# Layer one's a and b products in Strassen's form, fed by a list scheduler in the builder

## The chip, the core and the metric

The kernel runs on one core of one Trainium2 chip. TensorE (PE) multiplies matrices; VectorE (DVE), ScalarE (ACT) and GpSimd (POOL) do elementwise work; SyncE (SP) issues the DMAs. Each engine works through its own instructions in the order in which the program has them and waits at semaphores for the others. The metric is the device time of one execution in microseconds.

## The reference

Three stages follow each other, all in float32:

```python
# attention: batch 4, 8 heads, 576 tokens, head width 64
scores = scale * q @ k.T
scores = where(scores >= max(scores) - tau, scores, -1e9)
attn   = exp(scores - max) / (sum + 1e-9);  x = attn @ v      # x: 2304 x 512
# layer one: d_ff 1536
a = x @ w_a;  b = x @ w_b;  x = (a * b) @ w_out               # 2304 x 512
# layer two: d_ff 1024
h = x @ w_in;  sm = exp(h - max(h)) / sum;  s = h * sm
x = ((s - mean(s)) / sqrt(var(s) + 1e-6) * g_ln) @ w_out
```

## The kernel before

Every large float32 product runs in a rounded format that TensorE takes at one column per clock. Each operand is held as a high part (a rounded copy, made on ACT) and a low part (the operand minus the high part, made on DVE or POOL), and a product is the sum of three matmuls: high by high, high by low, low by high. So the a and b products of 128 features and n tokens are 2 x 4 x 3 = 24 matmuls n columns wide, and the y product (w_out) 4 x 3 = 12.

**Attention** runs in 72 steps of two score tiles, and six more in which the last tiles are worked off. A step's DVE scales the scores and takes their minimum (`ns`, L343), ACT takes the exponential (L355), POOL makes the threshold (`th`, L360), DVE masks and sums (L369), PE transposes (L389) and multiplies by v (L420). Single operations of other work are put between these by hand: the conversion of the first 15 weight pieces of 128x512 (L132, L135, L138 on DVE, L128 and L142 on ACT, the low part L145 on POOL), and the scaling and splitting of the first block of x. The x rows go to DRAM (`xd`) and come back by block.

**Layer one** walks over units of one token block by one block of 128 features (`units`, L644): four blocks of 512 tokens and one of 256 by twelve feature blocks, in two passes of six features. Per unit PE does the 24 a and b matmuls into one PSUM tile (`ab_mm`, L262) and the 12 y matmuls of the unit two before (`yacc`, L632, `LAG`). ACT copies a (L615), DVE multiplies by b (L616), ACT and DVE split the product (L617, L618). At the end of a pass ACT or DVE takes y out of PSUM (L636, L638); between the passes y waits in DRAM (`ypd`), x is stored once as `xsd` and read back and split again for the second pass. The remaining weight pieces are converted between the units in a fixed pattern (L661 to L666), and so are the 16 pieces of layer two.

**Layer two** takes 18 tiles of 128 tokens: `hid` (24 matmuls, L716), `chain` (softmax and variance on DVE and ACT), `lnt` (8 transposes L753, then L757 to L759) and `outp` (24 matmuls, L772). The input tiles are split on ACT and POOL (L594, L595).

Of the kernel before, what the change touches and what calls it, by code (L numbers as in the profile page):

```python
# [8 lines left out]
F32 = mybir.dt.float32  # L9
# [12 lines left out]
def kernel(  # L22
# [27 lines left out]
    NB = SM  # L50
    BLK = [[(b, 0, SM, 0)] for b in range(B)]
    BLK.insert(B - 1, [(b, SM, D, b * D) for b in range(B)])
    NBLK = len(BLK)
    LEN = [sum(n for _, _, n, _ in blk) for blk in BLK]
    TILES = [(j, c) for j in range(NBLK) for c in range(0, LEN[j], P)]
    NTILE = len(TILES)
    NW = 9
    F1 = 6
    LAG = 2
    RB = 2  # L60
    FW = 5
# [9 lines left out]
    xsd = [dram.tile([P, KC, n], F32, name=f"xsd{j}") for j, n in enumerate(LEN)]  # L71
    ypd = [dram.tile([P, KC, n], F32, name=f"ypd{j}") for j, n in enumerate(LEN)]
    yd = [dram.tile([P, KC, n], F32, name=f"yd{j}") for j, n in enumerate(LEN)]

# [9 lines left out]
    wstage = ctx.enter_context(tc.tile_pool(name="ws", bufs=2))  # L84
    xr_p = ctx.enter_context(tc.tile_pool(name="xr", bufs=1))
    xh_p = ctx.enter_context(tc.tile_pool(name="xh", bufs=1))
    ps_s = ctx.enter_context(tc.tile_pool(name="ps_s", bufs=2, space=PSUM))
    xs = {}
    vs = {}
    vnew = []  # L90
    pre = {}
    later = []
    xhs = [xh_p, None]
    wst = {}
    pools = {True: wpool}
# [24 lines left out]
    def conv_ops(stage):  # L120
        k = conv["k"]
        raw = conv["raw"].pop(k)
        n = raw.shape[1]
        w = {}

        def expo():
            w["f"] = stage.tile([P, n], F32, tag="w32", name="w32")
            nc.scalar.activation(out=w["f"], in_=raw[:, :, 1].bitcast(F32), func=AF.Abs, scale=2.0**-112)  # L128

        def low():  # L130
            w["l"] = stage.tile([P, n], U32, tag="wlow", name="wlow", bufs=1)
            nc.vector.tensor_scalar(out=w["l"], in0=raw[:, :, 0], scalar1=29, scalar2=None, op0=ALU.logical_shift_right)  # L132

        def sign():
            nc.vector.scalar_tensor_tensor(out=w["l"], in0=raw[:, :, 1], scalar=0x80000000, in1=w["l"], op0=ALU.bitwise_and, op1=ALU.bitwise_or)  # L135

        def join():
            nc.vector.scalar_tensor_tensor(out=w["f"].bitcast(U32), in0=w["f"].bitcast(U32), scalar=3, in1=w["l"], op0=ALU.logical_shift_left, op1=ALU.bitwise_or)  # L138

        def hi():  # L140
            w["o"] = conv_q[k][0]()
            nc.scalar.activation(out=w["o"][0], in_=w["f"] if wide else raw, func=AF.Copy)  # L142

        def lo():
            nc.gpsimd.tensor_tensor(out=w["o"][1], in0=w["f"] if wide else raw, in1=w["o"][0].bitcast(F32), op=ALU.subtract)  # L145

        return ([("A", expo), ("D", low), ("D", sign), ("D", join)] if wide else []) + [("A", hi), ("P", lo)]

    def conv_emit(stage, engs, count=1):
        while count and conv["k"] < min(conv["ld"], conv["lim"]):  # L150
            if not conv["ops"]:
                conv["ops"] = conv_ops(stage)
            if conv["ops"][0][0] not in engs:
                return
            conv["ops"].pop(0)[1]()
            count -= 1
            if not conv["ops"]:
                conv["k"] += 1

    def conv_step(stage):  # L160
        conv_load(stage)
        k = conv["k"]
        while conv["k"] == k and conv["k"] < conv["ld"]:
            conv_emit(stage, "ADP")

    def queue_w1(f):
        def piece(p):
            if p == 0:
                wst[f] = pools[f % NW < FW].tile([P, 3, 2, DM], F32R, tag="w", name=f"w1_{f}")
            return wst[f][:, p, 0], wst[f][:, p, 1]  # L170

        conv_pieces(piece, [w1[f, :, m] for m in range(3)])

    def queue_w2(i):
        def piece(p):
            g, p = divmod(i, 3)
            if p == 0:
                w2s[g] = pools[(NF + g) % NW < FW].tile([P, 3, 2, DM], F32R, tag="w", name=f"w2_{g}")
            return w2s[g][:, p, 0], w2s[g][:, p, 1]

        conv_pieces(piece, [w_in[:, i // 2, (i % 2) * 512:(i % 2 + 1) * 512] if i < 2 * KC else w_out[:, i - 2 * KC]])

    def load_x(j):
        n = LEN[j]
        xr = xr_p.tile([P, KC, NB], F32, name="xr0")[:, :, 0:n]
        zr = xr_p.tile([P, KC, NB], F32, name="zr")[:, :, 0:n]
        for b, s0, m, c in BLK[j]:
# [5 lines left out]
            for h in range(2):  # L193
                zs = rzd[b].rearrange("(k h) s -> h k s", h=2)[h:h + 1, :, s0:s0 + m]
                nc.sync.dma_start(out=zr[h * D:(h + 1) * D, :, c:c + m], in_=zs.to_broadcast([D, KC, m]))
        xs[j] = (xr, zr)

    def new_xt(j):
        return xhs[j % 2].tile([P, KC, 2, NB], F32R, name="xt")[:, :, :, 0:LEN[j]]

    normed = set()

    def norm_x(j, e):
        while vnew:
            b = vnew.pop()
            nc.vector.tensor_scalar(out=vs[b], in0=vs[b], scalar1=neg, scalar2=EPS / S, op0=ALU.mult, op1=ALU.mult)
        xr, zr = xs[j][:2]
        for b, _, m, o in BLK[j]:
            xe = xr[:, e, o:o + m]
            nc.vector.scalar_tensor_tensor(out=xe, in0=xe, scalar=vs[b][:, e, 0:1], in1=zr[:, e, o:o + m], op0=ALU.add, op1=ALU.mult)  # L210
        normed.add((j, e))

    def prep_x(j, st):
        if st == 0:
            xs[j] += (new_xt(j),)
        xr, zr, xt = xs[j]
        if st == 0:
            for e in range(KC):
                if (j, e) not in normed:
                    norm_x(j, e)  # L220
        for c in range(0, KC, 2):
            k = slice(c, c + 2)
            x0 = xr[:, k]
            if st == 0:
                nc.scalar.activation(out=xt[:, k, 0, :], in_=x0, func=AF.Copy)
            else:
                nc.vector.tensor_tensor(out=xt[:, k, 1, :], in0=x0, in1=xt[:, k, 0, :].bitcast(F32), op=ALU.subtract)
        if st == 1:
            later.append(lambda: nc.sync.dma_start(out=xsd[j], in_=xr))
            xs[j] = xt  # L230

    def prep_slots(j):
        xr, zr = xs[j]
        xt = new_xt(j)

        def high(e):
            nc.scalar.activation(out=xt[:, e, 0, :], in_=xr[:, e], func=AF.Copy)

        def low(e):
            nc.vector.tensor_tensor(out=xt[:, e, 1, :], in0=xr[:, e], in1=xt[:, e, 0, :].bitcast(F32), op=ALU.subtract)  # L240
            if e == KC - 1:
                later.append(lambda: nc.sync.dma_start(out=xsd[j], in_=xr))
                xs[j] = xt

        slots = []
        for c in range(0, KC, 2):
            slots += [(lambda e=e: norm_x(j, e), lambda e=e: high(e)) for e in range(c, c + 2)]
            slots += [(lambda e=e: low(e), None) for e in range(c, c + 2)]
        return slots

    def ab_mm(j, f):
        n = LEN[j]
        xt = xs[j]
        wt = wst[f]
# [18 lines left out]
    def prep_x2(j, c):  # L273
# [4 lines left out]
        if c + 2 == KC:  # L278
            xs[j] = xt
# [594 lines left out]
```

## Time and profile before

| | |
|---|---|
| time of three runs | 934.35, 933.31, 934.26 us; median 934.26 |
| the profiled execution | span 931.8 us (first to last instruction); 2.5 us below the median of the runs |
| attention | 0 to about 265 us |
| layer one | 264.88 to 711.92 us |
| layer two | 711.92 to 931.8 us |
| matmul instructions in the trace | 5680 |
| DMA | 95.46 MB, mean 102 GB/s |

The page gives the busy share of each engine over the span and in 40 slices, the clock that TensorE was granted, and the chain of work that ended last. The ends of matmuls are modelled, so a single matmul's duration is not its share of the time: what a matmul costs in a dense stream is the length of a piece of the chain divided by its count. Operations on the vector engines are read from their mean duration by shape.

### The profile page before, as it was taken

The page shows a single profiled execution, that of the slowest core. Times are in us where ns is not written, and L with a number is a line of the kernel's source. Part 1 is how long each engine was busy: PE and PEld are TensorE (multiplying, and loading weights), DVE is VectorE, ACT ScalarE, POOL GpSimd, SP SyncE. Part 2 cuts the span into 40 slices and gives each one's busy share as a digit, 9 for nine tenths or more (in the row PEclk, how much of TensorE's full clock was granted, in tenths as well). Part 3 has the DMA queues.
Part 4 walks back from the last instruction along what each step waited for, and adds up shares of the span by engine and source line. Part 5 has one row for each costly group of instructions (what it writes and reads, how often), then busy time and mean ns, then how long its engine had stood idle before and what let it go on. Part 6 is the DMA issues. An engine that isn't in the chain of part 4 may idle for free.

```text
span 931.8 us, 15032 instructions
## 1 busy us (share of the span) xinstructions
PE 919.4 (99%) x5680; PEld 704.5 (76%) x5680; DVE 538.2 (58%) x1169; ACT 438.5 (47%) x795; POOL 209.4 (22%) x292
## 2 busy tenths in 40 slices
PE   7999999999999999999999999999999999999998
PEld 3655555555578888889888888889988788888886
DVE  6999999999855243433266762223365544444443
ACT  5888888888743133333235432112232444444432
POOL 1233332333101002020023320000032433333330
PEclk9999999999999999999999999999999999999999
DMA  6445653367114334253126551122052111111100
GB/s 186 140 126 167 190 176 113 115 197 215 39 35 154 88 113 101 104 136 136 46 66 208 177 182 45 45 91 79 13 181 68 35 46 46 46 46 46 45 24 34
DMA packets 52904, 95.46 MB, mean 102 GB/s; under 512 B 12768, under 2 KB 29280, under 8 KB 50272
## 3 DMA queue, kind: packets, MB, share of 16 engines
q1 hardware_dynamic: 52032, 93.82, 31.9%
q8 instruction: 45, 0.74, 0.3%
q10 hardware_dynamic: 800, 0.68, 0.3%
q14 instruction: 27, 0.22, 0.1%
HBM read 70.80 MB, written 23.68 MB: 101 GB/s over the span
## 4 chain that ended last, share of the span: by engine, by line
PE 91%; DVE 5%; issue 1%; ACT 1%; DMA 0%; POOL 0%; ACTq 0%; POOLq 0%; DVEq 0%
PE ps L262 32%; PE py L632 16%; PE po L772 10%; PE ps L716 9%; PE po L420 8%; PE ps L338 7%; PE tp L389 7%; DVE ns L343 2%; PE pl L753 2%; DVE pe L369 1%; PE tq L405 1%; DVE e L728 0%; ACT e L727 0%; DMA taub<-in_tau_dram 0%; DVE nm L724 0%
## 5 line engine op out<-in xcount | busy, mean ns | idle before, releaser
L262 PE MATMUL ps<-xt,w 128*128 128x512 f32 (+1 forms) x1440 | 305.6, 368 | 0.0
L262 PEld LDWEIGHTS ps<-xt,w 128*128 128x128 f32 x1440 | 251.5, 189 | 45.0
L632 PE MATMUL py<-gt,w 128*128 128x512 f32 (+1 forms) x720 | 157.3, 368 | 0.0
L616 DVE TENSOR_TENSOR g<-ps,a 128x512 f32<-128x512 f32 (+1 forms) x60 | 38.3, 638 | 203.1 <-ACT a L615 203.1
L632 PEld LDWEIGHTS py<-gt,w 128*128 128x128 f32 x720 | 126.3, 189 | 22.5
L145 POOL TENSOR_TENSOR w<-w,w 128x512 fp32r<-128x512 f32 x52 | 76.9, 1479 | 283.5 <-ACT w L142 281.4
L615 ACT ACTIVATE a<-ps 128x512 f32<-128x512 f32 (+1 forms) x60 | 33.2, 554 | 193.0 <-PE ps L262 193.0
L355 ACT ACTIVATE pe<-ns,nm 128x576 f32<-128x576 f32 x128 | 94.0, 775 | 39.8 <-DVE ns L343 39.4
L343 DVE TENSOR_SCALAR_CACHE_REDUCE ns<-ps 128x576 f32<-128x576 f32 x144 | 103.0, 750 | 4.6 <-PE ps L338 4.4
L716 PE MATMUL ps<-w,ys 128*128 128x512 f32 x432 | 102.7, 393 | 1.6 <-POOL ys L595 1.4
L369 DVE SCALAR_TENSOR_TENSOR pe<-ns,th,pe 128x576 f32<-128x576 f32 x128 | 100.3, 813 | 5.1 <-ACT pe L355 2.8
L772 PE MATMUL po<-w,lt 128*128 128x512 f32 x432 | 101.4, 390 | 0.7 <-POOL lt L759 0.6
L338 PE MATMUL ps<-k,q 64*64 64x288 f32 x1152 | 90.8, 424 | 5.3 <-DMA k<-in_qkv_dram 3.4
L772 PEld LDWEIGHTS po<-w,lt 128*128 128x128 f32 x432 | 80.8, 188 | 18.1 <-POOL lt L759 1.1
L716 PEld LDWEIGHTS ps<-w,ys 128*128 128x128 f32 x432 | 79.8, 188 | 18.1 <-POOL ys L595 1.8
L360 POOL TENSOR_SCALAR th<-nm,toff 128x1 f32<-128x1 f32 x144 | 55.2, 386 | 157.2 <-DVE ns L343 152.2
L382 ACT ACTIVATE pt<-tp 128x512 f32<-128x512 f32 (+1 forms) x160 | 77.8, 545 | 0.7 <-PE tp L389 0.6
L420 PE MATMUL po<-pt,vr 128*64 128x322 f32 (+1 forms) x512 | 76.9, 419 | 0.5 <-ACT pt L382 0.4
L389 PEld LDWEIGHTS tp<-ident,pe 128*128 128x128 f32 x512 | 56.5, 143 | 23.8 <-issue 8.8
L389 PE MATMUL tp<-ident,pe 128*128 128x128 f32 x512 | 72.1, 280 | 0.2
L420 PEld LDWEIGHTS po<-pt,vr 128*64 128x64 f32 x512 | 32.2, 136 | 40.4 <-issue 17.2
L338 PEld LDWEIGHTS ps<-k,q 64*64 64x64 f32 x1152 | 36.9, 134 | 33.0 <-DVE ns L343 6.8
(74 smaller groups left out, 805.2 us busy)
## 6 DMA issues: line engine op xcount, KB each, us to landing
wraw<-in_w_dram SPq DMA_DIRECT2D x36, 512.0 KB
q<-in_qkv_dram SPq DMA_DIRECT2D x15, 576.0 KB
k<-in_qkv_dram SPq DMA_DIRECT2D x30, 176.0 KB
xd<-xp SPq DMA_DIRECT2D x16, 289.0 KB
y<-yd SPq DMA_DIRECT2D x18, 256.0 KB
vr<-in_v_dram SPq DMA_DIRECT2D x16, 256.0 KB
xr<-xd SPq DMA_DIRECT2D x4, 1024.0 KB
zr<-rzd SPq DMA_DIRECT2D x8, 512.0 KB
```

The source lines that it names most:

```text
L145: nc.gpsimd.tensor_tensor(out=w["o"][1], in0=w["f"] if wide else raw, in1=w["o"][0].bitcast(F32), op=ALU.subtract)
L262: nc.tensor.matmul(pa[:, 0:n], lhsT=wt[:, m, wi, kc * P:(kc + 1) * P], rhs=xt[:, kc, xi, :], start=(k == 0), stop=(k == 3 * KC - 1))
L338: nc.tensor.matmul(ps[t * D:(t + 1) * D, g, 0:HS], lhsT=q[r, u, c], rhs=k[r, u, o:o + HS], start=True, stop=True, skip_group_check=True)
L343: nc.vector.tensor_scalar(out=ns, in0=st[i, s][:, :, 0:HS], scalar1=-SCALE, scalar2=None, op0=ALU.mult, op1=ALU.min, accum_out=nm)
L355: nc.scalar.activation(out=pe.rearrange("p (g s) -> p g s", g=2), in_=ns, func=AF.Exp, bias=nm, scale=-1.0)
L369: nc.vector.scalar_tensor_tensor(out=pv, in0=ns, scalar=th, in1=pv, op0=ALU.is_le, op1=ALU.mult, accum_out=z[:, s:s + 1])
L382: evac_q.append(lambda: nc.scalar.activation(out=out, in_=in_, func=AF.Copy))
L389: nc.tensor.transpose(tp[:, kc, :], pe[:, o:o + P], ident)
L420: nc.tensor.matmul(po[h * D:(h + 1) * D], lhsT=lhsT, rhs=rhs, start=(kc == 0), stop=(kc == NQ), skip_group_check=True)
L632: nc.tensor.matmul(py, lhsT=wt[:, 2, wi, oc * P:(oc + 1) * P], rhs=gt[:, gi, :], start=(first and k == 0), stop=(last and k == 2))
L716: nc.tensor.matmul(ph[:, g, :], lhsT=y[:, a, kc, :], rhs=w2(2 * kc + g, b), start=(k == 0), stop=(k == 3 * KC - 1))
L772: nc.tensor.matmul(po, lhsT=lt[:, a, j, :], rhs=w2(2 * KC + j, b), start=(k == 0), stop=(k == 3 * NJ - 1))
```

## The change

The tokens are regrouped into three pairs of two halves of 384 tokens (`H`), the features into four passes of three blocks (`F1`). A unit is one pair by one feature block; there are 36, and the pairs run forward in even passes and backward in odd ones (`PAIRS`), so that the pair at a turn is kept.

In a unit the 2x2 problem (a and b by two token halves, with x cut into two halves of 256 rows) is done with seven products in place of eight. Each is 6 matmuls of 384 columns. Products 0, 3, 5 and 6 accumulate in one PSUM bank, 1 and 4 in a second, product 2 alone in a third; between them ACT copies the partial sums out (L951, L1008) and DVE adds them up (L1001, L1011, L1020). The two results a*b of the halves come from L1012 and L1029 and are split as before (L1018, L1021, L1032, L1033). The seven x operands are sums and differences made once per pair (`sum_ops`, `operand_ops`), stored in DRAM (`opd`) and read back when the pair comes again (`load_op`). The seven weight operands per feature block are made from differences of the converted pieces (`ab_tasks`).

The order on the engines of layer one comes from a list scheduler in the builder: it keeps a clock per engine with costs (`COST`, 0.1735 us per matmul of 384 columns, L182), and before each operation of the fixed chain it places those background tasks that would end early enough (`bg`, `crit`). Product 0 and 1 of the next unit stand before product 6 of the present one, and 24 y matmuls are spread over the gaps. In layer two `ys` of tiles 1 and 2 is made ahead, and `lnt(0)` stands before `chain(1)`.

```diff
-    NW = 9
-    F1 = 6
-    LAG = 2
+    H = NT // 6
+    NPR = NT // (2 * H)
...
+    F1 = 3
+    NPASS = NF // F1
+    NU = NPASS * NPR * F1
+    PAIRS = [p if q % 2 == 0 else NPR - 1 - p for q in range(NPASS) for p in range(NPR)]
...
+    opd = [[dram.tile([P, QK, 2, H], F32, name=f"opd{p}_{j}") for j in range(7)] for p in range(NPR)]
...
+    COST = {"A": (0.19, 0.83e-3), "D": (0.155, 1.04e-3), "P": (0.17, 2.17e-3), "S": (0.4, 0.0)}
...
+    def place(e, n, ready, sbuf):
+        s = max(clock[e], ready)
+        z = s + COST[e][0] + COST[e][1] * n * (e != "S")
+        if sbuf and n and e in port:
+            z += max(0.0, port["P" if e == "D" else "D"] - s - 0.1)
+        return s, z
...
+    def bg(limit, free_d=0.0, free_a=0.0, slack=0.5):
+        ends = {"D": limit + max(slack, free_d), "A": limit + max(slack, free_a)}
+        tasks[:] = sorted((t for t in tasks if t["ops"]), key=lambda t: t["due"])
...
+                        if s <= limit if e in "SP" else z <= ends[e]:
+                            got.append((s, t))
...
+    def crit(e, n, ready, fn, sbuf=False):
+        bg(ready)
+        _, z = place(e, n, ready, sbuf)
+        fn()
...
+        td = task(due - 7, [
+            diff(512, lambda: t()[:, 0:2], lambda: a()[:, 1], lambda: a()[:, :, 0, :]),
+            diff(256, lambda: t()[:, 2], lambda: a()[:, 1, 1], lambda: t()[:, 0]),
+            diff(256, lambda: t()[:, 3], lambda: a()[:, 0, 1], lambda: t()[:, 2]),
+        ], [tb])
...
+    def operand_ops(s, j, p):
+        def src():
+            return scs[s][:, (0, 0, 0, 1, 3, 2)[j]] if j in (1, 3, 4, 5) else quad(p, j // 6, min(j // 2, 1))
...
+    def load_op(s, j, p):
+        xts[s, j] = new_xt(s, j)
+        nc.sync.dma_start(out=xts[s, j].bitcast(F32), in_=opd[p][j])
...
+    def product(n, f, j):
+        ps = bank_of(n, BANK[j])
...
+        for c in range(QK):
+            for wi, xi in ACC:
+                nc.tensor.matmul(ps, lhsT=w[:, WOP[j], wi, c * P:(c + 1) * P], rhs=x[:, c, xi, :], start=(k == 0 and j < 3), stop=(k == 3 * QK - 1 and j in (2, 4, 6)), skip_group_check=True)
+                k += 1
...
+            free[n + 1, 1, 2] = tz[0] = crit("D", H, max(e2, tz[0]), lambda: nc.vector.tensor_tensor(out=tmp[0], in0=y, in1=tmp[0], op=ALU.add))
...
+            y_mm(4)
+            e3 = product(n, f, 3)
+            free[n, 0, 5] = tz[1] = crit("A", H, e3, lambda: nc.scalar.activation(out=tmp[1], in_=x, func=AF.Copy))
+            work(n, 1)
+            e4 = product(n, f, 4)
...
+            e5 = product(n, f, 5)
+            free[n, 0, 6] = tz[2] = crit("D", H, max(e5, tz[2]), lambda: nc.vector.tensor_tensor(out=tmp[2], in0=x, in1=tmp[2], op=ALU.add))
...
+            y_mm(6)
+            if n + 1 < NU:
+                fn = (n + 1) // F1 // NPR * F1 + (n + 1) % F1
+                nxt = first_copies(n + 1, (product(n + 1, fn, 0), product(n + 1, fn, 1)) if n else e01)
+            work(n, 5)
+            e6 = product(n, f, 6)
...
-            if t + 1 < NTILE:
-                split_y(t + 1, yp)
+            for k in (1, 2) if t == 0 else (t + 1,) if 1 < t < NTILE - 1 else ():
+                split_y(k, yp)
...
-            if t == NTILE - 1:
+            if t in (1, NTILE - 1):
                 lnt(t - 1)
```

Three places show how the instructions move. First PE in the steady part of layer one: before, one unit of 512 tokens (`ps` is the PSUM tile of a and b, `xt` the x block, `py` the y bank, `gt` the split product).

```order
L262 MATMUL ps<-xt,w_3_2160 128x512 x24
L632 MATMUL py<-gt,w_1_1149 128x512 x12
L262 MATMUL ps<-xt,w_4_3011 128x512 x24
L632 MATMUL py<-gt,w_2_1626 128x512 x12
```

After, a little more than one unit of 768 tokens (`acc` are the banks of a unit's products, `ga` and `gb` the split results of its two halves).

```order
L510 MATMUL acc_3966<-xt,w_4_4737 128x384 x6
L510 MATMUL acc_3969<-xt,w_4_4737 128x384 x6
L933 MATMUL py_3847<-ga,wo_4754 128x384 x2
L933 MATMUL py_3847<-ga,wo_4852 128x384 x3
L933 MATMUL py_3847<-ga,wo_4902 128x384 x3
L933 MATMUL py_3844<-gb,wo_4754 128x384 x3
L933 MATMUL py_3844<-gb,wo_4852 128x384 x3
L510 MATMUL acc_3966<-xt,w_4_4737 128x384 x6
L933 MATMUL py_3844<-gb,wo_4902 128x384 x3
L933 MATMUL py_3845<-gb,wo_4754 128x384 x3
L510 MATMUL acc_3967<-xt_5237,w_5_5001 128x384 x6
L510 MATMUL acc_3969<-xt_5237,w_5_5001 128x384 x6
```

The long runs of 24 and 12 became pieces of 6 and fewer, and all matmuls are 384 columns wide: 1512 for the products and 864 for y, where 1440 and 720 stood. The eighth row is product 5, which adds to the bank that L1008 copies after product 3 (the first row).

Second, PE at the start of layer one: before, with the last PV matmuls of attention (`po`) and the first units.

```order
L262 MATMUL ps<-xt,w_1_1149 128x512 x24
L262 MATMUL ps<-xt,w_2_1626 128x512 x24
L632 MATMUL py<-gt,w_0_672 128x512 x12
L262 MATMUL ps<-xt,w_3_2160 128x512 x24
L632 MATMUL py<-gt,w_1_1149 128x512 x12
```

After, from the same place (`py` banks serve as product banks in unit 0).

```order
L510 MATMUL py_3847<-xt,w_1_1324 128x384 x6
L510 MATMUL acc_3969<-xt,w_1_1324 128x384 x6
L510 MATMUL py_3844<-xt,w_0_852 128x384 x6
L510 MATMUL py_3845<-xt,w_0_852 128x384 x6
L510 MATMUL py_3844<-xt,w_0_852 128x384 x12
L510 MATMUL acc_3968<-xt,w_1_1324 128x384 x6
L510 MATMUL py_3847<-xt,w_1_1324 128x384 x6
L510 MATMUL acc_3969<-xt,w_1_1324 128x384 x6
L510 MATMUL py_3847<-xt,w_1_1324 128x384 x6
```

In the first three units no y matmul stands between the products; the fifth row is products 5 and 6 of unit 0 with nothing between them.

Third, DVE in the last units of layer one: before, a unit's two operations and the conversions between them.

```order
L616 TENSOR_TENSOR g_7001<-ps,a_7000 128x512
L618 TENSOR_TENSOR gt<-g_7001,gt 128x512
L138 SCALAR_TENSOR_TENSOR w_6966<-w_6966,wlow 128x512
L132 TENSOR_SCALAR wlow<-wraw 128x512
L135 SCALAR_TENSOR_TENSOR wlow<-wraw,wlow 128x512
```

After, one unit (`c` are the partial sums, `sc` and `wraw` belong to a weight piece of layer two, L907 takes y out of PSUM).

```order
L1001 TENSOR_TENSOR c_7571<-acc_3968,c_7571 128x384
L1033 TENSOR_TENSOR gb<-c_7469,gb 128x384
L907 TENSOR_TENSOR y_7526<-py_3846,y_7526 128x384
L225 SCALAR_TENSOR_TENSOR sc<-sc 128x512
L1011 TENSOR_TENSOR c_7572<-acc_3969,c_7572 128x384
L1012 TENSOR_TENSOR c_7571<-c_7571,c_7572 128x384
L907 TENSOR_TENSOR y_7551<-py_3847,y_7551 128x384
L218 TENSOR_SCALAR sc<-wraw 128x512
L1020 TENSOR_TENSOR c_7573<-acc_3966,c_7573 128x384
L1021 TENSOR_TENSOR ga<-c_7571,ga 128x384
L907 TENSOR_TENSOR y_7602<-py_3844,y_7602 128x384
L221 SCALAR_TENSOR_TENSOR sc<-wraw,sc 128x512
```

A unit has seven DVE operations of its own in place of two, and the conversions and y sums stand one by one between them.

## Rows read from the trace of the kernel before

**Rows 1.** The page: busy us, share and instructions; granted TensorE clock in 40 slices.

```profile
PE 919.4 (99%) x5680; PEld 704.5 (76%) x5680; DVE 538.2 (58%) x1169; ACT 438.5 (47%) x795; POOL 209.4 (22%) x292
...
PEclk9999999999999999999999999999999999999999
```

**Rows 2.** Busy time by stage: window, length, engines' busy us, clock, DMA share, GB/s.

```profile
8.65:264.88 256.23, 255.56 (x2476) 149.13 (x2476) 245.50 (x660) 212.87 (x413) 73.56 (x157) 1.00 0.48 147
274.00:712.00 438.00, 438.00 (x2137) 371.44 (x2136) 192.22 (x295) 138.06 (x235) 60.14 (x39) 1.00 0.32 106
712.00:931.80 219.80, 213.30 (x1008) 176.47 (x1006) 96.69 (x203) 83.59 (x142) 73.97 (x84) 1.00 0.15 46
```

**Rows 3.** The chain of waits, layer one: start us, us, engine, tile, line, count.

```profile
264.88 5.67 PE ps L262 x24
270.55 2.86 PE po L420 x20
273.42 0.21 PE rt L441
...
295.40 5.44 PE ps L262 x24
300.84 2.72 PE py L632 x12
...
429.51 2.88 PE ps L262 x24
432.39 1.44 PE py L632 x12
...
711.92 5.45 PE ps L716 x24
```

**Rows 4.** Groups by shape, 274 to 712 us: count, busy us, mean ns, idle before.

```profile
L262 PEld LDWEIGHTS ps<-xt,w 128*128 128x128 f32 x1413 | 246.6, 189 | 44.0
L145 POOL TENSOR_TENSOR w<-w,w 128x512 fp32r<-128x512 f32 x37 | 57.6, 1557 | 255.3 <-ACT w L142 255.3
L138 DVE SCALAR_TENSOR_TENSOR w<-w,wlow 128x512 uint32<-128x512 uint32 x37 | 38.0, 1026 | 1.9 <-ACT w L128 0.5
L618 DVE TENSOR_TENSOR gt<-g,gt 128x512 fp32r<-128x512 f32 x48 | 33.3, 693 | 33.5 <-ACT gt L617 33.5
L616 DVE TENSOR_TENSOR g<-ps,a 128x512 f32<-128x512 f32 x48 | 33.2, 692 | 175.7 <-ACT a L615 175.7
L135 DVE SCALAR_TENSOR_TENSOR wlow<-wraw,wlow 128x512 uint32<-128x512 uint32 x37 | 25.6, 693 | 1.3
L132 DVE TENSOR_SCALAR wlow<-wraw 128x512 uint32<-128x512 uint32 x37 | 15.8, 427 | 1.2
L618 DVE TENSOR_TENSOR gt<-g,gt 128x256 fp32r<-128x256 f32 x12 | 5.1, 426 | 5.8 <-ACT gt L617 5.8
L616 DVE TENSOR_TENSOR g<-ps,a 128x256 f32<-128x256 f32 x12 | 5.1, 424 | 27.3 <-ACT a L615 27.3
```

**Rows 5.** Weight loads where all matmuls are 256 wide, 425 to 437 us.

```profile
L262 PEld LDWEIGHTS ps<-xt,w 128*128 128x128 f32 x72 | 8.9, 192 | 0.0
```

**Rows 6.** Waits of PE in layer two, 712 to 932 us: total us, times, longest.

```profile
PE ps L716 <- POOL ys L595: 1.4, 1, 1.4
PE po L772 <- POOL lt L759: 0.6, 1, 0.6
```

**Rows 7.** Groups by shape in attention, 0 to 265 us on DVE, to 275 on POOL.

```profile
L138 DVE SCALAR_TENSOR_TENSOR w<-w,wlow 128x512 uint32<-128x512 uint32 x15 | 10.2, 679 | 0.0
...
L145 POOL TENSOR_TENSOR w<-w,w 128x512 fp32r<-128x512 f32 x15 | 19.3, 1286 | 28.2 <-ACT w L142 26.1 <-DVE ns L343 2.1
```

**Rows 8.** Single microseconds with a store of long rows, and with x and rz loads.

```profile
330.00:331.00 1.00, 1.00 (x6) 0.85 (x5) 0.00 (x0) 0.42 (x1) 1.00 (x1) 1.00 0.94 393
331.00:332.00 1.00, 1.00 (x6) 0.80 (x6) 0.00 (x0) 0.00 (x0) 0.24 (x1) 1.00 0.97 393
410.00:411.00 1.00, 1.00 (x10) 1.00 (x10) 0.93 (x3) 0.64 (x2) 0.00 (x0) 1.00 1.07 207
```

More of the change, by code (lines that the diff above doesn't have):

```diff
@@ new lines, in place, with commit, ready_of, transfer @@
+    def place(e, n, ready, sbuf):
[4 more added lines that the diff above has]
+        return s, z
+    def commit(e, z, sbuf):
+        clock[e] = z
+        if sbuf and e in port:
+            port[e] = z
+    def ready_of(t):
+        return max([t["end"], slot_at.get(t["ops"][0][3], 0.0)] + [d["end"] for d in t["deps"]])
+    def transfer(z, mb):
+        clock["Q"] = max(clock["Q"], z) + mb / RATE
+        return clock["Q"] + 2.0
@@ L140, in hi @@
-        def hi():
[L141 to L187, printed above, removed]
+            f = w["f"].bitcast(U32)
+            nc.vector.scalar_tensor_tensor(out=f, in0=f, scalar=3, in1=w["l"], op0=ALU.logical_shift_left, op1=ALU.bitwise_or)
+        if wide:
+            return [("A", 512, expo), ("D", 300, low), ("D", 512, sign), ("D", 512, join)]
+        return [("A", 512, lambda: nc.scalar.activation(out=dst(), in_=got["raw"], func=AF.Copy))]
@@ new lines, in whole_task, with part @@
+    def whole_task(src, tile_of, due, at, b, deps=(), free=None):
+        ld = load_w(src, due - 10, at - 16 if free is None else free, free is not None)
+        got = {}
+        def part(k):
+            if "b" not in got:
+                got["b"] = buffer(b)
+            return got["b"][:, k * DM:(k + 1) * DM]
+        t = task(due - 6, stage_ops(ld["got"], lambda: part(0), lambda: part(1)), [ld["load"]] + list(deps) + ([last[b]] if b in last else []), at - 12)
+        ld["used"] = t
+        last[b] = task(due, split_ops(tile_of, lambda: part(0), 512), [t], at)
+        return last[b]
@@ L192, in load_x @@
                 vnew.append(b)
[L193 to L249, printed above, removed]
@@ new lines, with bank_of, y_bank @@
+    ACC = ((0, 0), (0, 1), (1, 0))
+    WOP = (0, 3, 1, 5, 2, 4, 6)
+    BANK = (0, 2, 1, 0, 2, 0, 0)
+    bank = {}
+    free = {}
+    def bank_of(n, b):
+        if n == 0:
+            return bank["y"][(0, 2, 1)[b]][:, 0:H]
+        if n == 1 and b == 0:
+            return bank["y"][3][:, 0:H]
+        if "m" not in bank:
+            bank["m"] = [pools["ps"].tile([P, 512], F32, name=f"acc{k}", tag="tp") for k in range(4)]
+        return bank["m"][n % 2 if b == 0 else b + 1][:, 0:H]
+    def y_bank(i):
+        return bank["y"][i % 4][:, 0:H]
@@ L680, in moe1, with flush @@
+        def flush(every=False):
             for fn in later:
@@ L697, in moe2, with rest @@
+        for fn in lag:
+            fn()
+        slot["c"] = SL * (NU + 1)
+        for c in range(SL * NU, SL * (NU + 1) + 1):
+            slot_at[c] = clock["PE"]
+        while ysteps:
+            y_mm(9)
+            bg(clock["PE"])
+            flush()
+        flush(True)
+        es.close()
+        es_s.close()
+    def rest(left=None):
+        slot["c"] = SL * (NU + 9)
+        for t in sorted(tasks, key=lambda t: t["due"]):
+            force(t)
+    def moe2():
         es = ExitStack()
```

715 lines of the change are left out of this document (505 added, 210 removed).

## The prediction

> **What bounds the kernel now.** I read the page first: PE is busy for 99% of the span, at the full clock in all 40 slices [rows 1]. Since the ends of matmuls are modelled, that alone proves little, so the stages come next. In attention PE is busy for 255.56 of 256.23 us and DVE for 245.50; in layer one PE for all of 438.00 and DVE for 192.22; in layer two PE for 213.30 of 219.80 [rows 2]. The chain of waits then shows that layer one is nothing but matmuls: pieces of 24 and of 12 follow each other without a gap until layer two begins at 711.92 [rows 3]. So PE sets the time, what PE is given to do in layer one is what the change alters, and DVE has room there (44% busy).
>
> **PE's work in layer one.** A matmul of 512 columns costs 5.44 / 24 = 226.7 ns, one of 256 columns 2.88 / 24 = 120.0 ns; the pieces of y give the same, 2.72 / 12 and 1.44 / 12 [rows 3]. Four blocks of 512 tokens and one of 256, twelve features, 24 + 12 matmuls: 1728 x 226.7 + 432 x 120.0 ns = 391.7 + 51.8 = 443.5 us. The chain has 711.92 - 264.88 - 2.86 - 0.21 = 444.0, so the account closes.
>
> The changed kernel has 36 units of 7 x 6 = 42 product matmuls and 24 y matmuls, 2376 in all, each 384 columns wide. That width is not in the trace. From below, it costs at least what a column costs at 512, 226.7 x 0.75 = 170.0 ns; from above, at most what a column costs at 256, 120.0 x 1.5 = 180.0 ns. The two widths fit a constant part of 13 ns and 0.417 ns a column, which gives 173.3 ns; I take it, since 384 lies between the two rows it rests on. 2376 x 173.3 = 411.8 us, **31.7 us less** (39.6 less by the lower bound, 15.8 by the upper). The y matmuls alone stay at the same number of columns; the gain is the eighth product.
>
> **What the change puts on DVE and POOL, and what hides it.** Own DVE work per unit: four operations that read PSUM, between 692 and 424 ns, so 558 ns at 384, and three in SBUF, between 693 and 426, so 560 [rows 4]; over 36 units 80 + 60 us. 72 y sums of 558 ns: 40 us. 46 weight pieces of 427 + 693 + 1026 ns [rows 4]: 99 us. Weight differences, low parts and x operands that the order leaves to DVE, 21 of 512 columns' length, 12 of 256 and some ten longer ones: about 29 us. Together 309 of 411.8 us, 75%. POOL has 82 operations in layer one, as much as 82 of 512 columns; at 1557 ns [rows 4] 128 us, 31%. PE covers both as long as a result is there when PE comes to it. The two short covers are these: product 5 follows product 3's copy (ACT) behind product 4 and 14 y matmuls, 20 x 173 ns = 3.5 us; product 6 follows L1020 behind 6 y matmuls and two products of the next unit, 18 x 173 ns = 3.1 us. The add of 0.56 us leaves 2.5 us of the shorter cover. So in the steady part I cost the longer chain of sums at nothing, and keep 3 us for single late results and late loads over 36 units (0 to 20).
>
> **The start of layer one loses cover.** In the first three units no y matmul stands between the products. In unit 0 product 6 comes right behind 5, so it waits for the add, 0.56 us and the release; product 5 waits for ACT's copy behind one product only. Queued behind those waits on PE is everything, so they count in full: about 0.8 + 0.4 us, and a few tenths in units 1 and 2. The second pair's operands go through POOL then: thirteen operations, four low parts of weights (5.5 us), then nine sums and low parts of 768 columns' length (1557 x 1.5 = 2.3 us), 26 us in a row, against some 20 us until unit 3's first product and 13 more until its last; the first operand is out after 15, the last after 26. I take 2 us (0 to 8).
>
> **Attention.** The same PE work in the same order stands there, and PE had 0.7 us to spare in 256 [rows 2], so nothing can be won. DVE gets less to do: 15 pieces of three conversions (30 us) become 6 pieces and 16 scalings. POOL gets 17 operations for the first weights and 11 long ones for x between the thresholds; the masks and the next tile's scores are their cover. I take 0, with a bound of +6 (half a microsecond at each of the long ones). The three products at its end (18 x 173 = 3.1 us, where 5.67 stood [rows 3]) still outlast ACT's last copies; then 2.86 of PV follow as before.
>
> **Layer two** has the same matmuls. PE's wait for `ys` of tile 2 (1.4 us and its weight load's part) and for `lt` of tile 0 (0.6) [rows 6] should go, since both are made earlier: -2 (-3 to +3, the latter if layer two's last weight pieces, which are converted during the last y matmuls, hold up the first chain).
>
> **The sum,** against the profiled execution: 931.8 - 31.7 + 2 + 3 - 2 = 903.1 us of span. The runs' median lies 2.5 us above that execution, so the prediction is **906 us**; 898 to 914 by the bounds of the terms as they come most often.
>
> **The rivals.**
> *Late data, 921 us.* Passes two to four move 42 x 0.786 MB of x operands, 144 x 0.197 MB of y and 34 x 0.524 MB of weights, 79 MB in 27 units of 11.4 us: 256 GB/s, where layer one had 106 [rows 2]. Long rows went at 393 GB/s, broadcast rz with x at 207 [rows 8]. The operands have rows of 6 KB and are like the former; even with all y traffic at 207 the queue has 267 us of work in 308. But an operand's buffer comes free only one unit before its successor is needed. Six changes of operands at 3 us each, in place of the 3 us above: 906 - 3 + 18 = 921. Chance 0.10.
>
> *DVE and POOL exclude each other, 928 us.* DVE's L138 takes 679 ns in attention and 1026 in layer one, POOL's L145 1286 and 1557 [rows 4, 7]: each POOL operation there cost DVE about 0.35 us, which over 82 makes 309 + 28 = 337 us, still under PE. If every POOL operation stopped DVE for its whole length, DVE would need 309 + 128 = 437 us, 25 more than PE, and the time would be 906 - 3 + 25 = 928. The operations that read PSUM (120 us of the 309) speak against it: at 692 ns L616 is no longer than its SBUF neighbour. Chance 0.07. The Trainium skill (SBUF — State Buffer, Who interferes with whom) has it that the port pair DVE shares with GpSimd is an exclusive lock held for the whole instruction. By that rule this rival gains; the trace agrees in kind, with 347 ns where the whole operation would be 1557.
>
> *Slower: DVE is late at product 6 in every unit, 942 us.* The place is L1020. If two conversions stand before it and the first is caught behind a long POOL operation, 2.3 + 0.69 + 1.03 + 0.56 = 4.6 us pass where the cover is 3.1. That is 1.5 us of waiting; in 26 of 36 units it is 39 us: 906 - 3 + 39 = 942. It decides against the change from 31.7 / 36 = 0.9 us a unit on. For it: the order has four conversion operations a unit on average. Against: with 75% load a backlog must clear within the unit. Chance 0.06.
>
> *The weight load sets the pace, 943 us.* A load of 128x128 shows 189 ns [rows 4], more than 173. At 189 ns a matmul layer one would take 449 us, 6 more than now: 934.3 + 6 + 2 + 3 - 2 = 943. Against it: where all matmuls are 256 wide the loads show 192 ns [rows 5] and yet a matmul comes every 120. Chance 0.03.
>
> **How the numbers follow.** The forecast has 0.74; the four rivals 0.10, 0.07, 0.06 and 0.03. Faster by more than 0.2%, which is about what the measurement can tell: the forecast and the first two, less some overshoot, 0.89. Slower 0.09, the rest 0.02. For the range I take 896 to 928: down to the lower bound of the matmul with layer two's gain, up to the two middle rivals.
>
> **What would show it.** Right: in layer one the chain is made of L510 in pieces of 6 at 1.04 us and L933, its length is 412 to 420 us, and PE's longest waits stand in its first three units; layer two is 218 us long and attention ends within 3 us of 265. Wrong: DVE or POOL in the chain of the steady part, L1020 as what PE waits for, waits for `xt` from `opd`, a granted clock below full in some slice, or a matmul of 384 columns that costs 180 ns or more in a dense stretch.

## The result and the profile after

The changed kernel takes **946.34 us** (median of 4 runs, 946.07 to 947.08) against 934.31 us before in the same runs: a ratio of 1.013, 95% interval 1.0115 to 1.0144. The forecast was 906 us, faster; the kernel is slower. The profiled execution has a span of 944.8 us, 13.0 more than before.

The page of the changed kernel, to be held against [rows 1]: PE busy is down by 10.9 us, and the clock is no longer full in every slice.

```profile
PE 908.5 (96%) x5896; PEld 752.5 (80%) x5896; DVE 654.3 (69%) x1359; ACT 471.9 (50%) x886; POOL 283.0 (30%) x347
...
PEclk9999999999999898999999999999999899999999
```

Busy time by stage, changed kernel, columns as in [rows 2]: attention up to the first product of layer one, layer one, layer two, and 260 us out of the middle of layer one.

```profile
8.65:279.02 270.37, 261.89 (x2475) 149.59 (x2476) 248.32 (x637) 208.88 (x399) 90.85 (x170) 0.99 0.48 146
279.02:719.30 440.28, 426.56 (x2402) 422.87 (x2398) 300.18 (x503) 174.43 (x339) 113.42 (x79) 0.98 0.68 235
719.30:944.80 225.50, 216.53 (x1009) 178.89 (x1008) 103.20 (x212) 85.78 (x146) 77.05 (x86) 0.98 0.14 45
380.00:640.00 260.00, 260.00 (x1492) 260.00 (x1491) 176.87 (x310) 100.51 (x198) 52.61 (x44) 1.00 0.69 236
```

Against the stages of before (264.88; 447.0; 219.9 us, [rows 2, 3]) attention has got 14.1 us longer, layer one only 6.8 shorter, layer two 5.6 longer. From 380 to 640 us nothing is wrong: PE never stops. The chain of waits there (start, us, engine, tile, line, count) consists of products and y pieces alone, one unit every 11.51 us (28 units from 371.94 to 694.34 us):

```profile
417.98 4.16 PE acc L510 x24
422.83 2.08 PE acc L510 x12
424.91 2.43 PE py L933 x14
429.42 4.22 PE acc L510 x24
```

So the loss sits in three places, and the list of PE's waits (us in total, times, longest) names them: the masks of attention (L617), four entries in the first six units of layer one, and `rz` at the start of layer two. Left out are the first loads and, but for the second entry of L1020, what stays under 1.2 us in total.

```profile
PE acc L510 <- DVE xt L448: 5.6, 2, 3.5
PE tp L637 <- DVE pe L617: 5.2, 7, 1.6
PE pl L1125 <- DVE rz L1106: 4.9, 2, 4.7
PE py L933 <- DVE wo L236: 4.6, 1, 4.6
...
PE py L510 <- DVE c L1020: 2.7, 1, 2.7
...
PE acc L510 <- DVE c L1020: 0.8, 1, 0.8
```

**Attention.** The timeline of DVE and POOL in the changed kernel (start us, us, engine, line):

```profile
211.22 0.82 DVE L617 SCALAR_TENSOR_TENSOR pe<-ns,th,pe 128x576 f32<-128x576 f32 x1 [0.24 <-ACT pe L603]
211.38 2.36 POOL L448 TENSOR_TENSOR xt<-xr,xt 128x768 fp32r<-128x768 f32 x1
...
211.96 2.38 DVE L617 SCALAR_TENSOR_TENSOR pe<-ns,th,pe 128x576 f32<-128x576 f32 x1
...
214.28 0.75 DVE L591 TENSOR_SCALAR_CACHE_REDUCE ns<-ps 128x576 f32<-128x576 f32 x1
```

A mask (L617) takes 0.82 us, the next one 2.38: it ends just after POOL's operation. The read of PSUM (L591) keeps its 0.75 us wherever it stands. Nine of the eleven long POOL operations stretch a mask, by 1.56 us each, 14.0 us in all. The other two run beside PSUM reads. That this sum is what attention is longer is partly luck: in the five traces that share this attention it ends between 276.7 and 279.0 us, 11.8 to 14.1 us later than before. Five more masks, between 50 and 118 us, are stretched to 1.82 us beside POOL operations for the first weights:

```profile
57.65 1.78 POOL L236 TENSOR_TENSOR w<-st_t,w 128x512 fp32r<-128x512 f32 x1
...
58.22 1.82 DVE L617 SCALAR_TENSOR_TENSOR pe<-ns,th,pe 128x576 f32<-128x576 f32 x1
```

In the end they cost next to nothing: the 105th of the 144 masks (at 194 us) starts 0.9 us later than in the kernel before, the last one 14.2. Nor do the thresholds come late from POOL's fuller queue: DVE's masks waited 1.7 us for them in all, 2.4 in the kernel before. In the kernel before no mask was ever longer than 824 ns, though 15 POOL operations of 1.3 us ran among them; each began beside a read of PSUM and none met a mask. Five of them held up the conversion behind that read (L132): it took 0.97 to 1.19 us where it takes 0.42 alone.

**Start of layer one.** The same, with conversions and sums in the masks' place. Changed kernel, unit 0:

```profile
290.35 0.56 DVE L1012 TENSOR_TENSOR c<-c,c 128x384 f32<-128x384 f32 x1
290.41 2.16 POOL L420 TENSOR_TENSOR sc<-sc,xr 128x768 f32<-128x768 f32 x1
290.83 2.03 DVE L218 TENSOR_SCALAR st_a<-wraw 128x512 uint32<-128x512 uint32 x1
...
292.78 0.55 DVE L1020 TENSOR_TENSOR c<-py,c 128x384 f32<-128x384 f32 x1
...
293.38 0.69 PE L510 MATMUL py<-xt,w 128*128 128x384 f32 x1 [2.68 <-DVE c L1020]
```

L218 takes 0.42 us alone and 2.03 here; product 6 waits for L1020 behind it. PE's waits between 285 and 366 us add up to 13.6 us (2.7 + 0.8 + 4.6 + 5.6). These are five waits, the last entry being one of 3.5 and one of 2.1. Behind each of them but the one of 0.8 us PE runs at the lower of its two levels for a while; around the wait of 4.6 us (wait, the 11.6 us behind it, the 11 after that; the third number from the end is the granted clock, a mean over its levels of 1.2 and 2.4 GHz):

```profile
313.80:318.40 4.60, 0.05 (x1) 0.05 (x1) 3.90 (x4) 1.02 (x3) 3.34 (x2) 0.88 0.50 210
318.40:330.00 11.60, 11.60 (x52) 11.60 (x53) 6.19 (x12) 3.31 (x6) 0.00 (x0) 0.75 0.81 182
330.00:341.00 11.00, 11.00 (x65) 11.00 (x64) 9.44 (x17) 7.25 (x15) 2.53 (x2) 1.00 0.85 320
```

12 product matmuls took 3.84 us there where 2.08 is the rule. Layer one's 2376 matmuls at the steady 174.5 ns, PV and a transpose would be 417.7 us; it has 440.3, so the start lost 22.6: 13.6 of waits and 9.0 more, mostly in slow pieces like that one.

**Start of layer two**, changed kernel:

```profile
727.22 0.63 ACT L878 ACTIVATE ys<-y 128x512 fp32r<-128x512 f32 x1 [5.90 <-DMA y<-yd]
727.76 0.62 ACT L233 ACTIVATE w<-sc 128x512 fp32r<-128x512 f32 x1
728.28 0.62 ACT L233 ACTIVATE wo<-st_a 128x512 fp32r<-128x512 f32 x1
...
729.70 0.68 DVE L236 TENSOR_TENSOR wo<-st_a,wo 128x512 fp32r<-128x512 f32 x1
730.30 1.21 DVE L1096 TENSOR_REDUCE nm<-ps 128x1 f32<-128x1024 f32 x1
...
735.05 1.97 PE L1125 MATMUL pl<-ident,e 128*128 128x128 f32 x8 [4.67 <-DVE rz L1106]
```

ACT stands for 5.9 us at the split of tile 2's `y`, whose load landed late (SP's queue had stood for the last y sums' stores). Behind it wait two weight copies, behind these two subtractions in DVE's queue, and behind them the reduction of tile 0, whose scores PE had finished some 5 us earlier.

### The profile page after: what moved, and what is told of

The parts are those of the page before. It is cut to its first block, busy times and chain, and to the rows that moved or that the text cites. A ratio compares the mean times of both kernels' runs of the same rounds, so it can differ in the third digit from the quotient of the medians.

```text
span 944.8 us, 16336 instructions
## 1 busy us (share of the span) xinstructions
PE 908.5 (96%) x5896; PEld 752.5 (80%) x5896; DVE 654.3 (69%) x1359; ACT 471.9 (50%) x886; POOL 283.0 (30%) x347
## 4 chain that ended last, share of the span: by engine, by line
PE 87%; DVE 7%; DMA 2%; issue 1%; ACT 1%; ACTq 0%; SPq 0%; POOL 0%; DVEq 0%; POOLq 0%
PE acc L510 26%; PE py L933 15%; PE po L1144 10%; PE ps L1088 9%; PE po L668 8%; PE ps L586 8%; PE tp L637 7%; DVE pe L617 3%; PE pl L1125 2%; PE py L510 1%; DVE ns L591 1%; DMA yd<-y 1%; PE tq L653 1%; DMA q<-in_qkv_dram 1%; DVE xt L448 1%
## 5 line engine op out<-in xcount | busy, mean ns | idle before, releaser
L510 PE MATMUL acc<-xt,w 128*128 128x384 f32 x1446 | 275.4, 340 | 6.5 <-DVE xt L448 5.6
L510 PEld LDWEIGHTS acc<-xt,w 128*128 128x128 f32 x1446 | 258.8, 191 | 7.7 <-DVE xt L448 6.2
L617 DVE SCALAR_TENSOR_TENSOR pe<-ns,th,pe 128x576 f32<-128x576 f32 x128 | 117.7, 951 | 7.7 <-ACT pe L603 6.6
L591 DVE TENSOR_SCALAR_CACHE_REDUCE ns<-ps 128x576 f32<-128x576 f32 x144 | 103.2, 752 | 10.7 <-PE ps L586 10.2
L933 PE MATMUL py<-ga,wo 128*128 128x384 f32 x432 | 86.2, 340 | 4.6 <-DVE wo L236 4.6
L933 PE MATMUL py<-gb,wo 128*128 128x384 f32 x432 | 84.0, 334 | 0.0
L933 PEld LDWEIGHTS py<-ga,wo 128*128 128x128 f32 x432 | 77.7, 192 | 4.9 <-DVE wo L236 4.9
L951 ACT ACTIVATE c<-acc 128x384 f32<-128x384 f32 x69 | 33.8, 492 | 91.1 <-PE acc L510 69.0
L933 PEld LDWEIGHTS py<-gb,wo 128*128 128x128 f32 x432 | 75.7, 188 | 0.0
L1088 PE MATMUL ps<-w,ys 128*128 128x512 f32 x270 | 72.8, 401 | 0.0
L1096 DVE TENSOR_REDUCE nm<-ps 128x1 f32<-128x1024 f32 x18 | 22.0, 1223 | 59.3 <-PE ps L1088 59.1
```

Source lines behind the costliest of these rows:

```text
L510: nc.tensor.matmul(ps, lhsT=w[:, WOP[j], wi, c * P:(c + 1) * P], rhs=x[:, c, xi, :], start=(k == 0 and j < 3), stop=(k == 3 * QK - 1 and j ...
L591: nc.vector.tensor_scalar(out=ns, in0=st[i, s][:, :, 0:HS], scalar1=-SCALE, scalar2=None, op0=ALU.mult, op1=ALU.min, accum_out=nm)
L617: nc.vector.scalar_tensor_tensor(out=pv, in0=ns, scalar=th, in1=pv, op0=ALU.is_le, op1=ALU.mult, accum_out=z[:, s:s + 1])
L933: nc.tensor.matmul(g["py"], lhsT=wos[g["q"] * F1 + r][:, wi, oc * P:(oc + 1) * P], rhs=g["g"][r][:, gi, :], start=(r == c == 0), stop=last ...
L1088: nc.tensor.matmul(ph[:, g, :], lhsT=y[:, a, kc, :], rhs=w2(2 * kc + g, b), start=(k == 0), stop=(k == 3 * KC - 1))
```

## The experiments

The theory: a DVE operation whose operands lie in SBUF does not run while a long POOL operation runs; it waits for its end. One that takes an operand from PSUM does not wait. The rivals are given with each run. Ratios are to the kernel before on the same chip, with 95% intervals.

**b_pool**: the kernel before, with POOL operations that serve nothing.

```
 elif ch == "f":
+    if 56 <= m < 67:
+        nc.gpsimd.tensor_tensor(out=dum, in0=dum, in1=dum, op=ALU.subtract)
```

> The kernel before, with 11 subtractions of 768 columns added on POOL in attention, one a step from step 56 on, behind the thresholds, on a tile that nothing else uses (no data to wait for, no transfer). Theory (a DVE operation whose operands are all in SBUF does not run while a POOL operation of this kind runs, it waits to its end): each of the 11 stretches a mask from 0.81 to about 2.3 us, DVE passes most of it on to PE, attention gets 8 to 15 us longer, 943 to 950 us in all. Rival (in the changed kernel attention got longer because operands, x data or stores came late, or ACT had more to do): nothing of that is here, 934 to 937 us.

944.22 us, ratio 1.0108 [1.0093, 1.0123]: 10.2 us longer, with no data, transfer or ACT work added. One step of it on POOL's timeline, and then on DVE's:

```profile
213.54 1.97 POOL L552 TENSOR_TENSOR dum<-dum 128x768 f32<-128x768 f32 x1
```

DVE:

```profile
213.37 0.81 DVE L369 SCALAR_TENSOR_TENSOR pe<-ns,th,pe 128x576 f32<-128x576 f32 x1
...
214.11 2.01 DVE L369 SCALAR_TENSOR_TENSOR pe<-ns,th,pe 128x576 f32<-128x576 f32 x1
...
216.05 0.75 DVE L343 TENSOR_SCALAR_CACHE_REDUCE ns<-ps 128x576 f32<-128x576 f32 x1
```

Eleven masks are stretched, by 1.20 us each: 13.2 us, of which DVE's slack took 3.

**b_pool_gate**: as many elements on POOL, at another moment.

```
 evac_q, pv_q = [], []
+if 50 <= m < 72:
+    i1, s1 = cur[-1]
+    nc.gpsimd.tensor_scalar(out=gate, in0=st[i1, "z"][:, s1:s1 + 1], ...)
+    h = dum[:, m % 2 * 384:m % 2 * 384 + 384]
+    nc.gpsimd.tensor_tensor(out=h, in0=h, in1=h, op=ALU.subtract)
```

The first POOL operation reads `z`, the sum that the step's second mask writes.

> The kernel before, with the same elements on POOL as 22 subtractions of 384 columns, one a step from step 50 on, each behind a small POOL operation that reads what the step's second mask wrote, so that it runs beside the next step's reads of PSUM. Theory (exclusion between POOL and the masks alone): the masks stay at 0.81 us, attention is at most 3 us longer, 934 to 938 us. Rival (POOL's work or its traffic to SBUF costs DVE whenever it runs): 8 to 15 us longer, as without the wait, 943 to 950 us.

935.05 us, 1.0012 [1.0003, 1.0022]: 1.0 us. The list of the masks' line (shortest, median and longest in ns, first and last start) has none over 826 ns:

```profile
L369 DVE SCALAR_TENSOR_TENSOR pe<-ns,th,pe x128: 802/814/826, 8.8 to 262.2; 128x576 f32<-128x576 f32 x128
```

A subtraction on POOL, and DVE beside it:

```profile
210.84 0.83 POOL L580 TENSOR_TENSOR dum<-dum 128x384 f32<-128x384 f32 x1
...
211.12 0.75 DVE L343 TENSOR_SCALAR_CACHE_REDUCE ns<-ps 128x576 f32<-128x576 f32 x1
```

So it is not the work on POOL or its traffic that costs, but which DVE operation it stands beside. **b_pool_ts** replaced the subtraction by an operation that reads one tile:

> The kernel before with 11 POOL operations of 768 columns that read one tile (a multiplication and an addition with constants) in place of the subtractions of two tiles. If any POOL operation of that length excludes DVE, the masks beside it are stretched as far as POOL's operation is long; if only those that read two tiles do, the masks stay at 0.81 us and the time at 934 to 935 us.

937.62 us (one run). The POOL operation takes 1.40 to 1.48 us, and eleven masks are as long (the masks' line again):

```profile
L369 DVE SCALAR_TENSOR_TENSOR pe<-ns,th,pe x128: 799/814/1453, 8.6 to 265.1; 128x576 f32<-128x576 f32 x128
```

The Trainium skill (SBUF — State Buffer, Who interferes with whom) says that a DVE instruction with two SBUF inputs contends with a GpSimd instruction that reads SBUF, one with at most one SBUF input outside the two-port modes does not, and that the second of two that contend is blocked until the first has finished. The masks (2.01 us beside 1.97, 1.45 beside 1.40) and the PSUM reads (0.75 throughout) agree with it.

**a_gate**: the changed kernel with the same cure in attention.

```
+                        if cur and slots[0][0] == "DP":
+                            break
...
+            if m >= 52 and cur and slots and slots[0][0] == "DP":
+                i1, s1 = cur[-1]
+                nc.gpsimd.tensor_scalar(out=gate, in0=st[i1, "z"][:, s1:s1 + 1], ...)
...
+                    fn("P", slice(0, 1))
+                    slots.insert(0, ("DP", 1, lambda e, fn=fn: fn(e, slice(1, 2))))
```

The long operations are no longer issued behind the thresholds but after the masks, one half a step, and their order (`SLOTS`) is changed a little.

> The changed kernel with attention's 11 long POOL operations cut into halves, one a step, each behind the step's second mask; all else is as it was, but the second pair's x is loaded some steps later. Theory: attention's last product group starts at 265 to 269 us instead of 279; the start of layer one stays as it was or loses a few us to the later x; 931 to 939 us. Rival (attention is longer for the amount of work or for late data): 944 us or more.

951.61 us, 1.0186 [1.0171, 1.0201], longer instead of shorter. Attention did what was expected: the first products start at 265.5 us instead of 279.0. But one half a step takes until the end of attention, the second pair's x is loaded that much later, and PE waits at once:

```profile
290.45 2.29 PE L510 MATMUL py<-xt,w 128*128 128x384 f32 x6 [14.06 <-ACT c L1020]
298.54 1.97 PE L510 MATMUL py<-xt,w 128*128 128x384 f32 x5 [5.79 <-DVE c L1032]
```

I had expected "a few us" of that; the two waits are 20 us, and layer one is 459.0 us long instead of 440.3.

**a_plan**: the same, but done as early as in the changed kernel.

```
+        PLAN = {52: "n0", ..., 56: "s0 h0", 57: "l00 h1", 58: "s1 l01", ...,
+                ..., 64: "d4 l31", ..., 66: "l51 z0", 67: "o5 l60", 68: "l61 x0", 69: "o6"}
```

Here `s` is a sum, whole, on DVE, `d` the one low part on DVE, and `l` half a low part on POOL behind the step's second mask.

> The changed kernel with attention's work on the first pair's operands placed otherwise: the four sums and one low part on DVE, whole, the other six low parts on POOL in halves, each behind a step's second mask; so the second pair's x is loaded as early as in the changed kernel. Theory (exclusion in attention): masks stay at 0.81 us, attention's last products start at 265 to 269 us and the start of layer one is no later for it: 932 to 937 us. Rival (the first pair's work costs attention this time wherever it is put, since DVE has no room for it): 942 us or more.

933.75 us, 1.0006 [0.9992, 1.0020]; first products at 266.1 us, layer one 438.8 us long, within 1.5 us of the changed kernel's. None of the masks beside the twelve halves is stretched. So 12.6 us of the changed kernel's loss were these eleven operations' places.

**l1_dve**: no sums, differences or low parts on POOL in layer one.

```
 for t in tasks:
+    if e == "P" and t["ops"] and len(t["ops"][0][0]) > 1:
+        continue
...
+engs = engs[:1] if True else engs        # where a task is forced: DVE
```

> The changed kernel with every sum, difference and low part of layer one on DVE (POOL keeps two multiplications and layer two's own); attention as it was. Theory (POOL's operations hold DVE's up, each for longer than DVE would need for the same work): PE's waits in layer one's first six units fall from 13.7 us to under 6, DVE is busy for about 90% of the steady part, which may cost a few us there; 932 to 942 us. Rival (DVE simply has too much in a row in the first six units, and the weight and operand pieces are late for that): more waits there, 948 us or more.

929.17 us, 0.9954 [0.9937, 0.9970]: 17 us less than the changed kernel and less than I expected; layer one is 424.6 us instead of 440.3, and PE's waits at its start are 4.3 us instead of 13.6. The steady part shows why that is free. The same 260 us as above:

```profile
380.00:640.00 260.00, 260.00 (x1493) 260.00 (x1492) 182.58 (x348) 95.33 (x187) 0.00 (x0) 1.00 0.72 250
```

POOL's 52.6 us of work there had shortened DVE's busy time by only 5.7 us (182.58 - 176.87). The rest came back as waiting: the groups by shape in that stretch (count, busy us, mean ns, idle) have the product of two SBUF tiles in each unit (L1012 there, L1015 here) at, in the changed kernel,

```profile
L1012 DVE TENSOR_TENSOR c<-c,c 128x384 f32<-128x384 f32 x23 | 21.7, 945 | 0.6
```

and here,

```profile
L1015 DVE TENSOR_TENSOR c<-c,c 128x384 f32<-128x384 f32 x23 | 12.8, 556 | 0.6
```

while L1020, which reads PSUM, has 555 and 556 ns. DVE is busy for 70% of that stretch and 75% of layer one (316.9 of 424.6 us), not the 90% that I expected. A part of this, 46 x (1026 - 688) ns = 16 us of layer one, is that the forecast's 309 us took L138's stretched mean of [rows 4] for work (the same conversion, L228 here, takes 688 ns); the rest was not followed.

**l1_dve36** does the same in the first six units alone (`slot["c"] < 36`).

> The changed kernel with all sums, differences and low parts on DVE in layer one's first six units alone; from then on POOL takes its share as in the changed kernel. Theory (POOL's long operations in a row at the start are what costs; later PE covers them): the same time as with all of layer one on DVE, 927 to 931 us. Rival (the gain of that kernel came from the steady part too): 935 us or more.

933.11 us, 0.9993 [0.9979, 1.0008], between the two. Layer one is 428.5 us, so 11.8 of the 15.7 us come from the first six units; both the forecast (927 to 931) and the rival (935) missed. The other 3.9 us of layer one hold one more wait for L1020 (1.4 us). In the profiled run, slower than the median, layer two is also 3.0 us longer than in l1_dve, with a longer wait for `rz` (5.5 against 3.2). How the later POOL operations move these was not followed.

**l1_half** keeps the work on POOL and cuts it: x sums and low parts of layer one as two instructions of 384 columns each.

> The changed kernel with POOL's sums and low parts of x in layer one as two instructions of 384 columns each where one of 768 stood; the same work on POOL at the same places. Theory (a DVE operation waits for the POOL operation that runs, so its wait is as long as what is left of that one): a wait is at most about 1.1 us instead of 2.1, PE's waits in the first six units fall from 13.7 to about 8 us, 936 to 941 us. Rival (POOL's whole time counts, however it is cut, since the next half follows at once): 944 to 948 us.

935.98 us, 1.0023 [1.0011, 1.0034], 10.4 us less than the changed kernel; layer one 431.3 us. PE's waits in its start are 8.1 us in place of 13.6:

```profile
PE acc L512 <- DVE xt L450: 3.6, 2, 2.1
PE py L935 <- DVE wo L236: 2.6, 1, 2.6
PE py L512 <- DVE c L1022: 1.9, 1, 1.9
```

DVE gets its turn between two halves: the L218 that took 2.03 us ahead of product 6 takes 1.22 here.

```profile
288.49 1.22 DVE L218 TENSOR_SCALAR st_a<-wraw 128x512 uint32<-128x512 uint32 x1
```

So the length of one POOL instruction goes into the size of a wait.

**l2_order** changes one thing in layer two.

```
 for k in (1, 2) if t == 0 else (t + 1,) if 1 < t < NTILE - 1 else ():
+    if k == 2:
+        rest()            # the last weight pieces
     split_y(k, yp)
-if t == 0:
-    rest()
```

> The changed kernel with one thing in another order at the start of layer two: the last weight pieces are issued ahead of the split of tile 2's y, whose load lands late. Theory (that split stands ahead of two weight copies in ACT's queue, these hold up two subtractions in DVE's queue, and behind them the first tile's reduction waits): PE's wait of 4.7 us for rz shrinks to about 1.5, with the slow clock behind it; 941 to 944 us. Rival (the reduction is late for DVE's y sums and the late y data themselves): no change, 946 us.

941.43 us, 1.0085 [1.0070, 1.0100]. Layer two falls from 225.5 to 222.1 us, the wait for `rz` from 4.7 to 2.1 us. The rest of the 4.9 us lies ahead of it, where both kernels do the same: among those that share its attention, that stage ends anywhere from 276.7 to 279.0 us.

**best1** has a_plan, l1_dve and l2_order together.

> All three at once: attention's work placed otherwise, layer one's sums, differences and low parts on DVE, layer two's last weight pieces ahead of tile 2's split. If the three losses are separate, their gains add: 946 - 12 - 17 - 3 = 914 us (910 to 919). Rival (what attention wins is lost again in the first units, because the second pair's operands are then late): 922 us or more.

**914.41 us**, 0.9799 [0.9783, 0.9816]: faster than both kernels. The three losses add. By stage:

```profile
8.65:266.40 257.75, 257.22 (x2475) 149.44 (x2467) 236.58 (x638) 207.54 (x399) 83.62 (x184) 1.00 0.50 150
266.40:692.95 426.55, 420.58 (x2402) 417.20 (x2398) 318.86 (x580) 174.42 (x340) 11.29 (x7) 1.00 0.71 245
692.95:912.10 219.15, 214.28 (x1009) 176.82 (x1008) 102.14 (x212) 85.50 (x145) 75.28 (x85) 1.00 0.14 45
```

Attention is 1.5 us longer than before, layer one 20.5 shorter, layer two 0.7 shorter. What is left in layer one's start is 6 us of waits and the slow clock behind the longest of them (2.2 us).

**best2** moves the first three `wo` tiles' due times (`8 + f` to `2 + f`).

> The kernel with all three corrections, and the due times of the first three third-weight tiles earlier by six slots, so that their low parts are made ahead of the second pair's operands. In the corrected kernel PE still waits 1.6 us for these weights, with a stretch at the lower clock behind it. If that wait goes and no operand gets late for it: 910 to 913 us. Rival (the operands of unit 3 are late instead): 914 us or more.

916.41 us (913.05 to 919.08), 0.9808 [0.9780, 0.9836]: no gain. In the profiled run, the fastest of the four, the wait for `wo` went and 5.4 us of waits for `xt` came (2.1 the longest), as the rival had it.

## Why the prediction was wrong

**What bounds the kernel** was read rightly, and so was **PE's work in layer one**: 173.3 ns a matmul were forecast, a unit of 66 takes 11.51 us, 174.5 ns. The rival of the weight load is gone with it, though its rows still show 188 ns. **Late data** did not come in the steady part at 236 GB/s; it came at the start of layer two (ACT's 5.9 us for `y`) and in a_gate.

**The step that failed first is Attention**: "I take 0, with a bound of +6 (half a microsecond at each of the long ones)", with "the masks and the next tile's scores are their cover". It was +14.1. The masks are no cover for such an operation; they are what it stops, for 1.56 us and not 0.5, on an engine that [rows 2] shows busy for 245.5 of 256 us. b_pool reproduces 10 of the 14 us without the change, a_plan takes 12.6 away with the change in. The 17 operations for the first weights stretched five masks too, but there DVE had room again before 194 us.

**The start of layer one**, 2 us (0 to 8), came to 22.6. The mechanism was named at its place: product 6 behind L1020, and a conversion caught behind a long POOL operation, even with the right length (2.3 us). But I put that into the rival of all units, where a load of 75% spoke against it, and priced the start by the queue lengths alone. The slow clock behind the waits, up to 9 us, was in no term. Two of the prediction's own signs of being wrong showed it: L1020 among PE's waits, and slices below the full clock. Of the 22.6, l1_dve takes 15.7 away; in the other 6.9 its trace still has 4.3 us of waits.

**Layer two**, -2, came to +5.6. The two waits that were to go did go: neither `ys` nor `lt` is among PE's waits. But I counted only the tiles that are ready earlier and not what stands ahead of tile 0's reduction in ACT's and DVE's queues; the 4.7 us for `rz` came instead, and PE is busy 3.2 us longer in layer two (216.53 against 213.30), with a granted clock of 0.77 from 735 to 747 us. l2_order takes 3.4 of it away.

**The rival "DVE and POOL exclude each other"** had the right cause and the wrong sum. It added POOL's time to DVE's over all of layer one and found 25 us of overload. There is none: POOL's operations stretch DVE, and PE covers that through 30 units. The price falls due where DVE's results have no cover: in attention and in the first six units. The counter-argument, that operations with a PSUM operand are not stretched, was true and did not speak against it, since the masks have none. And the hint in [rows 4, 7], L138 at 1026 against 679 ns, was a mean: of the 37 operations 23 took 0.68 or 0.69 us, and 14 that met a POOL operation 1.34 to 1.79, most as long as it. The kernel before already showed the whole wait:

```profile
477.89 1.59 POOL L145 TENSOR_TENSOR w<-w,w 128x512 fp32r<-128x512 f32 x1 [60.66 <-ACT w L142]
...
478.44 1.59 DVE L138 SCALAR_TENSOR_TENSOR w<-w,wlow 128x512 uint32<-128x512 uint32 x1
```

Stage by stage, by the profiled runs: -31.7 forecast for the matmuls, -29.4 measured (2376 x 174.5 ns); 0, +14.1; +5 for start and stray waits, +22.6; -2, +5.6. The four measured terms make +12.9, and the span grew by 13.0; they are stages of the same trace, so this only shows that none is left out.

## What to carry to other kernels

Where POOL is to take work off DVE, look first at which DVE operations will stand beside it: in these traces those that read PSUM run on and those that live in SBUF wait for its end, so an operation of 2 us on POOL that spares 0.95 us on DVE can lose twice. Give such an operation a moment (a dependence on the last DVE operation that it would stop), a short length, or give it back to DVE; here all three worked, as long as the work did not come later for it (a_gate). A load averaged over a long stage says nothing about its first units: price starts and ends of a stage by the order in each queue there, and add the slow clock behind PE's longer waits.

## What the runs showed of the hardware

POOL's own time includes its turn: the same 768 columns took 1.86 us with DVE idle or at PSUM, and 2.36 where a mask was under way when it was issued. A shift of 32-bit integers from SBUF to SBUF on DVE (L218, one tensor read) is held up like the operations that read two: 2.03 us for 0.42. And PE's waits cost part of their length once more, in matmuls at the lower clock behind them: 9.0 on top of 13.6 us at the start of layer one, where the waits of 2.1 to 4.6 us were followed by it and the one of 0.8 us was not. In best1 the wait of 2.2 us was followed by 4 us of it (granted clock 0.50 from 281 to 284 us), those of 1.4 us and less by none.
